# Where the last product of a triple stands in TensorE's order: a gated recurrence followed by a SwiGLU block

## The chip, the cores and the metric

The kernel runs on one core of one Trainium2 chip. The metric is the device time of one execution in microseconds (us); lower is better. TensorE does the matrix products and writes them to PSUM banks, VectorE (DVE in the profile) and ScalarE (ACT) read the banks and do the elementwise work, GpSimd (POOL) and SyncE (SP) mostly issue transfers.

## The reference, cut to what matters

Two layers follow each other. The first is a recurrence over 768 steps for 4 batches of 8 heads, with a state of 48 by 48 per head; the second is a gated feed-forward block over all 3072 tokens.

```python
f = 1 / (1 + exp(-f_logit))                       # (4, 8, 768, 48)
for t in range(768):
    state = f[t, :, None] * state + k[t] v[t]^T
    y[t]  = q[t] @ state
x = y as (3072, 384)
g = x @ w_gate                                    # (384, 1536)
out = (g * sigmoid(g) * (x @ w_val)) @ w_out      # (1536, 384)
```

## The kernel before, in words

The 768 steps are cut into six chunks of 128, so that there are 24 **attention units**, one for each batch and chunk. The feed-forward block takes one chunk of all four batches (512 tokens) at a time. The first chunk goes through plain matrix products; the chunks 1 to 5 go through `mlp_fifteen`, and this is where the change lies. I call the work of `mlp_fifteen(c)` **block c**. In the profile block 1 runs from about 137 to 233 us, block 2 to 327, block 3 to 419, block 4 to 509 and block 5 to the end.

In a block the product with `w_gate` and `w_val` is made by a fast algorithm: both matrices are split in three by three parts, the tokens in three by two, and fifteen products of sums of parts replace eighteen. One **triple** makes those fifteen products for one of four column groups (`NJ` is 4), so a block has four triples, taken in the order 0, 2, 1, 3. Each **product** (`product(r)`, line 1061, r from 0 to 14) is two matrix multiplications of 128x128 by 256 in fp32; a profile shows them as four MATMUL rows and four LDWEIGHTS rows. I write r13 for the product with r = 13, and r0' for the first product of the next triple.

The products go to PSUM tiles by name, as the list `PRODUCTS` says: products 0, 3, 6, 9, 12 and 14 go to one bank "A" and add up there, 1, 4, 7, 10 and 13 to "B", and "o" and "c" take the rest. Between two products that add up in one bank, ScalarE copies the bank out (line 1066: the tiles `c11`, `c22`, `aside` and so on), because each partial sum is needed. VectorE then adds and subtracts these copies (lines 960 and 963). At the end of each of six sums, ScalarE takes the Silu of the gate half (line 1077) and VectorE multiplies it with the value half (line 1013); the products with "A" in the last sum are read from the bank itself. These `finish` steps are put off into the next triple, and those of a block's last triple are made by `finish_late`. Three pools concern us: "A" has two banks, "B" one, and "o" two, which "c" shares; attention units have three banks of their own.

The end of a triple reads

```python
                ("A", "a32", "t11"), ("B", "e1", "t3"), ("A", "a22", "b21")]   # r12, r13, r14
...
                elif r == 12:
                    lag(minus, got[31], got[31], aside("A"))
```

so r14 adds to the bank that r12 wrote, and must come after the copy `aside("A")` of r12. Only r13 lies between.

After the four triples, a block does the product with `w_out` by another fast algorithm of seven products (`down_seven`: `one`, `six`, `two`, `three`, `four`, `five`, `seven`, line 1160, the last at line 1223). Each comes in two halves; a half of `six` is six matrix multiplications of 128x128 by 192, which the profile shows as twelve rows. The first half of `one` or of `six` reads only the hidden tiles of the first two triples.

The order on each engine is written out by hand. `in_turn_of_time` walks over the steps of a block, each with its deemed duration (`PRODUCT` 0.86, half of `DOWN` 1.95), and ahead of a step it puts in every waiting piece whose time has come. `in_order` then fixes this order on each engine. The waiting pieces are those of the attention units of chunk c + 1, with times given by `SCORES`, `CHAINS` and `times`. At a unit's score time these come at once: a Sigmoid of the next unit's gates on ScalarE (line 619), the outputs of the unit before (tiles `y`, lines 745 and 752, and `dS`, line 794), and the scores of the unit itself (tile `sc`, line 701). The scores need two banks, of the pool that `SCORES` names, and VectorE frees them with the causal mask (line 723). Earlier pieces of a unit include the second scan (line 681), the transposition of q (line 685) and the product that gives `qT` (line 593).

A score time `between[n]` falls at the boundary ahead of triple n (counted in order of time), behind r14 of the triple before it.

Of the kernel before, what the change touches and what calls it, by code (L numbers as in the profile page):

```python
# [290 lines left out]
def short_path(ctx, tc, ident, least, judge, q, k, v, f_logit, moe_w_gate, moe_w_val, moe_w_out, out):  # L291
# [12 lines left out]
    NCH = S // C  # L304
# [597 lines left out]
    NJ = NG // 128  # L902

    PRODUCT, DOWN, PLAIN, PLAIN_DOWN = 0.86, 3.9, 2.57, 2.65
# [7 lines left out]
    def chain(k, q, qmul, turn=None, head=None):  # L912
        return (*[k + t for t in STEPS], turn or k + 3.5, head or k + 3.5, q, qmul)

    whole = NJ * TRIPLE + 7 * DOWN
    between = [n * TRIPLE - 0.05 for n in range(NJ)]
    down = [NJ * TRIPLE + n * DOWN / 2 - 0.05 for n in range(14)]
    SCORES = {c: scores for c, scores in zip(range(2, NCH), (
        ((12, "b"), (between[2], "o"), (down[2], "A"), (down[5], "A")),
        ((PRODUCT - 0.05, "b"), (between[1], "o"), (between[3], "o"), (down[3], "A")),  # L920
        *[((down[10] - whole, "A"), (between[1], "o"), (between[3], "o"), (down[3], "A"))] * (NCH - 4)))}
    CHAINS = {c: chains for c, chains in zip(range(2, NCH), (
        (chain(2.6, 4, 8.6), chain(14.5, 20, 23), chain(30, 37, 43.2), chain(57.4, 57.8, 61)),
        (chain(-12, -8.5, -5), chain(3.5, 6, 9), chain(16, 28, 33, 21.5, 23.5), chain(40.1, 53, 55, 44.5, 52)),
        *[(chain(-19.4, -11.2, -9.5), (-7.5, -6.3, 1.3, 2.2, 3.2, 5.5, 8, 10), chain(16, 28, 33, 21.5, 23.5), chain(40.1, 53, 55, 44.5, 52))] * (NCH - 4)))}
    LAST = 72.5

    def times(c):
        at = [t for t, _ in SCORES[c]]
        outputs = [*at[1:], down[10] if c + 1 in SCORES and SCORES[c + 1][0][0] < -1 else LAST]  # L930
        sigmoid = [-14 if c == 3 else SCORES[c - 1][-1][0] - whole - 0.01 if c > 3 else 0, -1.5 if c == 3 else at[0] - 0.01, *[t - 0.01 for t in at[1:]]]
        masks = {"b": 2, "o": 0.9, "A": 1.5}
        return [[f, *steps, s + 0.02, s + masks[kind], s + 2.2, o, o + 0.01, o + 2.1]
                for f, steps, (s, kind), o in zip(sigmoid, CHAINS[c], SCORES[c], outputs)]
# [56 lines left out]
    def down_weight_sums():  # L991
# [4 lines left out]
        for i in (1, 2, 4):  # L996
# [7 lines left out]
    PRODUCTS = [("A", "a11", "t14"), ("B", "a23", "t8"), ("o", "a21", "b22"),  # L1004
                ("A", "a12", "t2"), ("B", "e3", "b32"), ("o", "e0", "t1"),
                ("A", "e5", "t9"), ("B", "e2", "t5"), ("c", "a13", "b11"),
                ("A", "e4", "t4"), ("B", "a33", "t15"), ("c", "a31", "t10"),
                ("A", "a32", "t11"), ("B", "e1", "t3"), ("A", "a22", "b21")]
# [3 lines left out]
    def lag(f, *args):  # L1012
        lagging.append(lambda: f(*args))  # L1013

    def mlp_fifteen(c):
# [113 lines left out]
        hidden_sums, last = down_seven(c, h)  # L1129
        order = list(range(0, NJ, 2)) + list(range(1, NJ, 2))  # L1130
        pieces = [f for j in order for f in triple(j)]
        half = len(PRODUCTS) * (NJ // 2)
        pieces.insert(half + 12, (0, lambda: lag(hidden_sums, 0)))
        pieces += [(0, finish_late), last[0], (0, lambda: lag(hidden_sums, 1))]
        return token_sums, pieces + last[1:]

# [211 lines left out]
    def tokens_of(c):  # L1348
        token_sums, blocks[c] = mlp_fifteen(c)
        token_sums()  # L1350
# [9 lines left out]
def kernel(  # L1360
# [22 lines left out]
    def judge(bank):  # L1383
# [13 lines left out]
        yield  # L1397

    short_path(tc, ident, least, judge, *args)
    with tc.If(redo[0] > 0, label="redo"):  # L1400
        general_path(tc, *args)
# [32 lines left out]
```

## Time and profile before

| quantity | value |
|---|---|
| median of 3 runs | 595.06 us (595.02 to 595.18) |
| the profiled execution's own time | 595.19 us |
| its span in the profile | 593.5 us |
| granted TensorE clock | 0.998 |
| TensorE busy with matmuls, busy with weight loads | 98%, 81% of the span |
| VectorE, ScalarE, GpSimd busy | 80%, 51%, 19% of the span |

A profile row gives an engine, a line of the kernel, an operation, and the tiles out<-in. PE is TensorE's matmul, PEld its weight load, which runs beside the matmul ahead of it. A matmul's start is measured; its end is modelled, so the durations of neighbours overlap. What one product costs is therefore read from the start of one group to the start of the next. "DVE x <- ACT y: 5.0, 19, 0.3" in the list of waits means that DVE stood idle ahead of work on x 19 times, for 5.0 us in all and 0.3 us at most, until ACT had finished y.

### The profile page before, as it was taken

How to read it: one execution, taken by the hardware profiler on the slowest of the kernel's cores; microseconds unless marked ns; L12 is line 12 of the kernel's file. 1: busy time of each engine (PE TensorE's matmuls, PEld its weight loads, DVE VectorE, ACT ScalarE, POOL GpSimd, SP SyncE). 2: the span in 40 equal slices, each digit the busy share in tenths (PEclk: the TensorE clock that was granted, in tenths of full speed). 3: DMA queues.
4: the chain of work that ended last, by engine and by line, in shares of the span. 5: the costliest groups of instructions: out<-in, count | busy, mean ns of one | idle time of the engine just before them, and what ended most of it. 6: DMA issues, size and time to landing. Idle time of an engine off the chain costs nothing.

```text
span 593.5 us, 11514 instructions
## 1 busy us (share of the span) xinstructions
PE 583.6 (98%) x4292; PEld 480.6 (81%) x4292; DVE 477.1 (80%) x826; ACT 303.2 (51%) x567; POOL 112.2 (19%) x240
## 2 busy tenths in 40 slices
PE   8899999999999999999999999999999999999996
PEld 5744445667888999888899888899988899988896
DVE  7978898999989877998986988994978971666631
ACT  3588686024877422676640666631476730355600
POOL 3140345202132240111130030330030330000000
PEclk9999999999999999999999999999999999999999
DMA  9999597333666565552445332544230100100001
GB/s 193 266 309 263 167 229 171 64 99 107 120 120 110 93 149 138 130 109 65 88 117 137 100 81 63 103 109 113 81 92 27 29 11 6 54 1 2 2 0 57
DMA packets 106294, 61.91 MB, mean 104 GB/s; under 512 B 64200, under 2 KB 97032, under 8 KB 106232
## 3 DMA queue, kind: packets, MB, share of 16 engines
q1 hardware_dynamic: 93800, 45.96, 31.8%
q0 software_dynamic: 10992, 13.19, 10.0%
q10 hardware_dynamic: 1440, 1.97, 0.9%
q8 instruction: 35, 0.57, 0.4%
q14 instruction: 27, 0.22, 0.1%
HBM read 47.64 MB, written 8.13 MB: 94 GB/s over the span
## 4 chain that ended last, share of the span: by engine, by line
PE 96%; DVE 2%; ACT 0%; issue 0%; DMA 0%; ACTq 0%; DVEq 0%
PE o L1160 19%; PE A L1061 18%; PE B L1061 15%; PE o L1061 6%; PE c L1061 6%; PE o L868 5%; PE gate L845 5%; PE val L845 5%; PE o L1223 3%; PE sc L701 3%; PE y L745 2%; PE y L774 2%; PE dS L794 2%; PE y L752 1%; PE sc L704 1%; PE kt L708 1%
## 5 line engine op out<-in xcount | busy, mean ns | idle before, releaser
L763 POOL DMA_DIRECT2D xT<-yT x120 | 59.6, 504 | 66.6 <-ACT yT L756 51.4
L1061 PE MATMUL A<-xs,w_both 128*128 128x256 f32 x240 | 62.2, 382 | 0.0
L1160 PE MATMUL o<-w_out,h 128*128 128x192 f32 x360 | 62.0, 327 | 0.0
L1160 PEld LDWEIGHTS o<-w_out,h 128*128 128x128 f32 x360 | 58.7, 190 | 1.2 <-issue 0.7
L1066 ACT COPY aside<-A 128x512 f32<-128x512 f32 x60 | 35.1, 585 | 33.0 <-PE A L1061 32.7
L1066 ACT COPY c<-A 128x512 f32<-128x512 f32 x40 | 23.3, 582 | 55.8 <-PE A L1061 55.8
L960 DVE TENSOR_TENSOR c<-c,aside 128x512 f32<-128x512 f32 x60 | 41.1, 685 | 12.7 <-ACT aside L1066 11.1
L1061 PEld LDWEIGHTS A<-xs,w_both 128*128 128x128 f32 x240 | 44.9, 190 | 6.9 <-issue 1.0
L1013 DVE TENSOR_TENSOR h<-h,c 128x256 f32<-128x256 f32 x100 | 40.5, 413 | 7.6 <-ACT h L1077 7.3
L963 DVE TENSOR_TENSOR c<-c,aside 128x512 f32<-128x512 f32 x60 | 40.9, 682 | 2.8 <-ACT aside L1066 2.8
L1077 ACT ACTIVATE h<-c 128x256 f32<-128x256 f32 x100 | 39.4, 417 | 5.0 <-DVE c L960 3.8
L1160 PE MATMUL o<-ws,h 128*128 128x192 f32 x240 | 41.5, 328 | 0.0
L1061 PE MATMUL B<-xs,w_both 128*128 128x256 f32 x160 | 41.3, 380 | 0.0
L1061 PE MATMUL A<-xs,extra 128*128 128x256 f32 x160 | 41.2, 380 | 0.0
L1061 PE MATMUL B<-xT,extra 128*128 128x256 f32 x160 | 41.1, 379 | 0.0
L1061 PE MATMUL c<-xT,w_both 128*128 128x256 f32 x160 | 41.1, 379 | 0.0
L723 DVE TENSOR_TENSOR A<-sc,causal 128x512 f32<-128x512 f32 x48 | 30.8, 681 | 11.9 <-PE sc L701 11.6
L1066 ACT COPY aside<-B 128x512 f32<-128x512 f32 x60 | 35.1, 585 | 9.0 <-PE B L1061 7.0
L1160 PEld LDWEIGHTS o<-ws,h 128*128 128x128 f32 x240 | 39.1, 190 | 0.7 <-issue 0.7
L963 DVE TENSOR_TENSOR c<-o,c 128x512 f32<-128x512 f32 x40 | 27.3, 684 | 10.9 <-ACT h L1077 6.2
L960 DVE TENSOR_TENSOR c<-c,o 128x384 f32<-128x384 f32 x15 | 8.2, 548 | 34.4 <-PE o L1160 34.4
L1061 PEld LDWEIGHTS B<-xs,w_both 128*128 128x128 f32 x160 | 30.2, 190 | 4.6 <-ACT c L1066 0.4
(165 smaller groups left out, 1211.2 us busy)
## 6 DMA issues: line engine op xcount, KB each, us to landing
fsquares<-in_f_logit_dram SPq DMA_DIRECT2D x64, 96.0 KB, 4.0
qsquares<-in_q_dram SPq DMA_DIRECT2D x64, 96.0 KB, 2.4
ksquares<-in_k_dram SPq DMA_DIRECT2D x64, 96.0 KB, 2.5
w<-in_moe_w_gate_dram SPq DMA_DIRECT2D x6, 768.0 KB
w<-in_moe_w_val_dram SPq DMA_DIRECT2D x6, 768.0 KB, 6.2
w<-in_moe_w_out_dram SPq DMA_DIRECT2D x6, 768.0 KB, 8.4
v<-in_v_dram SPq DMA_DIRECT2D x19, 192.0 KB, 2.9
turn<-ksquares SPq DMA_DIRECT2D x40, 64.0 KB, 2.2
```

The source lines that it names most:

```text
L701: nc.tensor.matmul(sc[par][W * half:W * half + W, a * C:(a + 1) * C], lhsT=kT[r, a, W * half:W * half + W], rhs=qT[r, a, :], start=True, s ...
L723: nc.vector.tensor_tensor(A[:, par], sc[par].rearrange("p (a t) -> p a t", t=C), causal.unsqueeze(1).broadcast_to((128, HP, C)), ALU.mult)
L763: (nc.gpsimd if c >= SQUARES else nc.sync).dma_start(out=xT[c][f % 128:f % 128 + n, f // 128, b * C:(b + 1) * C], in_=yT[r:r + n, par, a / ...
L845: nc.tensor.matmul(p, lhsT=w[:, j, i, :], rhs=xT[c][:, i, :], start=(i == 0), stop=(i == KT - 1))
L868: nc.tensor.matmul(p, lhsT=hidden_tile(h, n // 2)[:, n % 2 * 2 + b // 2, b % 2 * C:(b % 2 + 1) * C], rhs=w_out[:, j, :], start=(n == 0), s ...
L960: nc.vector.tensor_tensor(dst, a, b, ALU.add)
L963: nc.vector.tensor_tensor(dst, a, b, ALU.subtract)
L1013: lagging.append(lambda: f(*args))
L1061: nc.tensor.matmul(p[name][:, n, :], lhsT=weights_of[a][:, n, j, :], rhs=tokens[b], start=fresh and n == 0, stop=True, skip_group_check=True)
L1066: nc.scalar.copy(t, p[name])
L1077: nc.scalar.activation(dst, src[:, 0, :], AF.Silu)
L1160: nc.tensor.matmul(p[:, n, :], lhsT=lhsTs[j][:, n * C:(n + 1) * C], rhs=rhs[:, j, :], start=first and j == order[0] and n == 0, stop=j == ...
```

## The change

It reorders TensorE's work at the ends of triples; no product, copy or transfer is added or removed. At a boundary after n triples that `APART[c]` names, r14 of the old triple and r0' change places. At five boundaries the score time moves from `between[n]` to `inside[n]`, one product earlier, so that the attention unit's matmuls come ahead of r14 and not behind it. At the end of the triples of blocks 2 to 5, the first half of `six` is taken out of the list of the `w_out` halves and put ahead of the last r14.

```diff
     between = [n * TRIPLE - 0.05 for n in range(NJ)]
+    inside = [t - PRODUCT for t in between]
     down = [NJ * TRIPLE + n * DOWN / 2 - 0.05 for n in range(14)]
     SCORES = {c: scores for c, scores in zip(range(2, NCH), (
         ((12, "b"), (between[2], "o"), (down[2], "A"), (down[5], "A")),
-        ((PRODUCT - 0.05, "b"), (between[1], "o"), (between[3], "o"), (down[3], "A")),
-        *[((down[10] - whole, "A"), (between[1], "o"), (between[3], "o"), (down[3], "A"))] * (NCH - 4)))}
+        ((PRODUCT - 0.05, "b"), (between[1], "o"), (inside[3], "o"), (down[3], "A")),
+        *[((down[10] - whole, "A"), (inside[1], "o"), (inside[3], "o"), (down[3], "A"))] * (NCH - 4)))}
...
     LAST = 72.5
+    APART = {1: (1, 3), 2: (1, 2), **{c: (2,) for c in range(3, NCH - 1)}, NCH - 1: range(1, NJ)}
...
         pieces = [f for j in order for f in triple(j)]
-        half = len(PRODUCTS) * (NJ // 2)
-        pieces.insert(half + 12, (0, lambda: lag(hidden_sums, 0)))
+        for n in APART[c]:
+            at = n * len(PRODUCTS)
+            pieces[at - 1], pieces[at] = pieces[at], pieces[at - 1]
+        pieces.insert(len(PRODUCTS) * (NJ // 2) + 12, (0, lambda: lag(hidden_sums, 0)))
+        if c > 1:
+            pieces.insert(-1, last.pop(2))
         pieces += [(0, finish_late), last[0], (0, lambda: lag(hidden_sums, 1))]
         return token_sums, pieces + last[1:]
```

The rows of `SCORES` belong to chunks 2, 3 and then 4 and 5, whose units run in blocks 1, 2, 3 and 4. Block 5 has no attention unit.

## The prediction

> **What bounds the kernel now.** I read the page's busy shares and its chain first.
>
> ```profile
> PE 583.6 (98%) x4292; PEld 480.6 (81%) x4292; DVE 477.1 (80%) x826; ACT 303.2 (51%) x567; POOL 112.2 (19%) x240
> ...
> PE 96%; DVE 2%; ACT 0%; issue 0%; DMA 0%; ACTq 0%; DVEq 0%
> ```
>
> TensorE has nearly all of the chain, so whatever it loses the end loses, and other engines matter only where TensorE waits for them. As matmul ends are modelled, 98% can hide short losses; the weight loads show them. The list of waits, for the weight loads alone, has one line that concerns the products:
>
> ```profile
> PEld A L1061 <- ACT aside L1066: 5.0, 19, 0.3
> ```
>
> The trace has these 19 waits, all ahead of r14: one per triple except the first of block 1. The timeline of one boundary (block 2, third triple next) shows PE, then PEld, then ACT:
>
> ```profile
> 251.02 1.03 PE L1061 MATMUL B<-xs,w_both 128*128 128x256 f32 x4
> ...
> 260.52 1.03 PE L1061 MATMUL A<-xs,w_both 128*128 128x256 f32 x4
> 261.38 1.03 PE L1061 MATMUL B<-xT,extra 128*128 128x256 f32 x4
> 262.28 1.13 PE L1061 MATMUL A<-xT,w_both 128*128 128x256 f32 x4
> 263.25 1.03 PE L1061 MATMUL A<-xs,w_both 128*128 128x256 f32 x4
> ```
> ```profile
> 261.17 0.84 PEld L1061 LDWEIGHTS B<-xT,extra 128*128 128x128 f32 x4
> 262.28 0.73 PEld L1061 LDWEIGHTS A<-xT,w_both 128*128 128x128 f32 x4 [0.27 <-ACT aside L1066]
> ```
> ```profile
> 261.64 0.59 ACT L1066 COPY aside<-A 128x512 f32<-128x512 f32 x1 [0.82 <-PE A L1061]
> ```
>
> Here r12, r13, r14, r0' start at 260.52, 261.38, 262.28, 263.25. ACT was idle, began the copy of r12 as soon as r12 was done, and ended at 262.23; only then did r14's load begin. r13's load had a lead of 0.21 us over its matmul, r14's none.
>
> **The price of one wait.** From 251.02 (r1) to 261.38 (r13) are twelve products: 10.36/12 = 0.863 us each. r13 and r14 together take 263.25 - 261.38 = 1.87. Other boundaries show 1.86 as well (181.24 to 183.10, 546.10 to 547.96), so I take 1.862 - 2 x 0.863 = 0.135 us: about 0.03 is r14's late start, and 0.105 is its slow first step. This, not the 0.27 us of the load's idle time, is what TensorE loses, since a load normally runs 0.21 us ahead.
>
> **What the Trainium skill says.** "TensorE: Matmul & The Clock Gate", section "Step-by-step: what each phase is for": TensorE pulls a weight load ahead of matmuls in flight, while matmuls stay in order. The trace agrees: 0.21 us of lead, lost when the load waits. "PSUM — Partial Sum Buffer", section "Terms": two engines may not be on the same bank and quadrant at once. That is why r14 must wait for a reader of bank A though it adds to it; the trace shows the wait. "ScalarE: Activation LUTs", section "What ACT_TABLE_LOAD costs", gives about 1.283 us for a table load; the table loads for Silu have exactly 1283 ns here.
>
> **The change, part by part.** Of the 19 waits I go through those that it touches.
>
> Plain swaps: block 1 before its fourth triple; block 2 before its second and third; blocks 3 and 4 before the third; block 5 before the third and fourth. That is 1 + 2 + 2 + 2 = 7 waits. With r0' between, r14 comes 1.73 us after r12's end, and the copy needs about 0.85 (261.38 to 262.23). r0' needs the other bank A, last read by DVE's multiplication (line 1013): of the first triple in block 2 that ends at 260.22, and r0' is wanted at 262.25, so 2.0 us are left (2.5 in block 1, where it ends at 179.58). r0' brings ScalarE one more copy (c11, 0.58 us) ahead of r14, and r14 has none, so r1' finds bank B two products after r13, as before. I cost the swap at nothing on this cover; if it failed, the cost would be up to the 0.135 gained. At block 2's second triple the unit stays between r0' and r14.
>
> Unit ahead of r14: one boundary in block 2, two each in blocks 3 and 4: 5 waits. TensorE's changes of shape stay the same in number. The first product after scores is dear anyway, because its load has no lead:
>
> ```profile
> 249.07 1.05 PE L701 MATMUL sc<-qT,kT 48*64 48x128 f32 x32
> 250.06 1.13 PE L1061 MATMUL A<-xs,w_both 128*128 128x256 f32 x4
> 251.02 1.03 PE L1061 MATMUL B<-xs,w_both 128*128 128x256 f32 x4
> ```
>
> that is 0.96 for r0'. Now r14 pays this 0.10 and r0' doesn't, and r14's own 0.135 goes. The unit issues all its work 1.0 us earlier: y, dS and scores on PE, the Sigmoid and two yT copies on ACT, six xT transfers on POOL, and the v load and mostly one kt transfer on SP. r14 has no such work, so it is moved past nothing on ACT, POOL and SP. Two things could be late. The scores need bank "o", freed by DVE's subtraction from c, which ends at 338.86 and 431.44 ahead of the second triple of blocks 3 and 4, while scores would start about 340.6 and 432.7; the least slack is 1.2 us. qT is ready even earlier. And yT may wait for the Sigmoid behind a table load (1.28 + 0.63 us), about 0.5 us; nothing on PE waits for it soon.
>
> Half of `six` ahead of r14: blocks 2 to 5, 4 waits. PE has the same rows; a product beside w_out rows costs no more than usual (block 4 enters its first product at 419.11 after 24 rows from 415.21, 3.90 us as elsewhere). The half issues nothing to other engines. What moves with it is DVE's order in blocks 2 to 4: the second scan and the transposition of q, due at 52 and 53, now come ahead of the last triple's multiplications. At the end of block 2 DVE does now:
>
> ```profile
> 292.38 0.69 DVE L960 TENSOR_TENSOR c<-c,aside 128x512 f32<-128x512 f32 x1
> 293.56 1.09 DVE L1013 TENSOR_TENSOR h<-h,c 128x256 f32<-128x256 f32 x3 [0.48 <-ACT h L1077]
> 294.57 0.41 DVE L1013 TENSOR_TENSOR h<-h,A 128x256 f32<-128x256 f32 x1
> 294.90 1.23 DVE L681 TENSOR_TENSOR_SCAN gates<-gates,start 128x516 f32<-128x516 f32 x1
> 296.04 0.68 DVE L685 STREAM_TRANSPOSE tails<-qsquares 128x512 f32<-128x512 f32 x1
> ```
>
> After the change: sum to 293.07, scan and transposition (1.23 + 0.68) to about 294.9, first multiplication to 295.3. Its tile is wanted by the second half of `one`, in its second third. That half starts at 291.57 + 1.95 + 0.86 + 1.95 = 296.3, the third at 297.0, its load at 296.8: 1.5 us of slack. Bank A of r14 is read later, but its next user, the scores before the second half of `six`, comes 3.9 us after r14. The transposition's q load is issued with the transfers of a unit earlier, some 20 us ahead by the schedule, so SP is no cover that could go.
>
> The first swap in block 1 gains nothing: scores and the kt transposition already lie ahead of r14 there, and r14 takes one usual step:
>
> ```profile
> 152.12 1.03 PE L1061 MATMUL A<-xT,w_both 128*128 128x256 f32 x4
> 152.99 1.03 PE L1061 MATMUL A<-xs,w_both 128*128 128x256 f32 x4
> ```
>
> Block 5's first swap meets the small `row` transposition ahead of r14: it sits inside the wait today, and must be paid by itself then (0.11 us by its start-to-start), so I count 0, with 0.13 as the upper end. Two waits in block 1 (third triple, end) stay.
>
> **Sum.** (7 + 5 + 4) x 0.135 = 2.16 us. The profiled execution took 595.19 (span 593.5 and 1.7 around it) and would take 593.0; it stood 0.13 above the median of 595.06, so for a median I say 595.06 - 2.16 = **592.9 us**.
>
> **The rivals.** First, the new places take waits of their own in the nine boundaries with an attention unit or w_out: then only the swaps pay, 7 x 0.135 = 0.95, time 594.1. For it speaks that DVE is busy 82.0 of 93 us in block 1 and 81.5 of 94 in block 2; against it the slacks of 1.2 us and more. Second, the change doesn't do what it says: the slow first step belongs to r14 itself, and only the late start of 0.03 goes: 16 x 0.03 = 0.5, time 594.6. The 0.87 us of r14 at 152.12 speaks against it. Third, on the other side: DVE becomes the bound at the ends of blocks 2 to 4. The scan and transposition stand ahead of the multiplications, and if DVE reaches them late, `one` stops for its hidden tile. It starts to cost once DVE is 1.5 us later than worked out and ends slower than before by 0.2% once that is 2.6 us, (2.16 + 1.19)/3 beyond the slack. If the slack is gone altogether, three blocks pay 1.91 us each: 592.9 + 5.7 = 598.6. For it speaks the strict order in DVE's queue; against it that the same pieces run now without a wait before them.
>
> **How the numbers follow.** A measurement of this kernel can tell about 0.2%, 1.19 us, from no change. All sixteen waits go: 0.86, with 592.3 to 593.5 as its own range (the two ends are `row` and some 0.4 us of three other products that wait for a ScalarE copy in block 1's second triple, and a quarter of the gain lost). Only the swaps pay: 0.05. Only late starts go: 0.03. DVE at the block ends: 0.06. The first is faster by over 0.2%, the next two within it, the last slower: 0.86, 0.08, 0.06. The range reaches from 592.3 to the swaps' case, 594.2.
>
> **What would show it.** In the profile after, the line of waits for `aside` should fall from 19 to two of 0.27 us and perhaps one short one; r14 behind r0' should take 0.863 and behind scores 0.97; PE should show the same rows. A new PEld wait of r0' on a multiplication, of `sc` on a subtraction or of `o` on `h` would show the rivals, and a span that shrinks by less than 1.2 us would make the forecast wrong.

## The result, and the profile after

The changed kernel takes 592.87 us (median of 6 runs, 592.80 to 593.02), the kernel before, run again beside it, 595.08 (594.97 to 595.26). The ratio is 0.9963, with a 95% interval of 0.9950 to 0.9976. The profiled execution took 593.02, with a span of 591.3 at a granted clock of 0.999.

The page's busy shares and chain look as before:

```profile
PE 580.7 (98%) x4292; PEld 481.9 (81%) x4292; DVE 477.4 (81%) x826; ACT 302.8 (51%) x567; POOL 112.3 (19%) x240
...
PE 96%; DVE 2%; DMA 1%; ACT 0%; issue 0%; SPq 0%; ACTq 0%; DVEq 0%
```

TensorE has the same 4292 rows and the same share of a shorter span. The shares can't tell where the time went. The list of waits of the weight loads can (us in all, times, longest):

```profile
PEld A L1063 <- ACT yT L756: 0.7, 4, 0.2
...
PEld A L1063 <- ACT aside L1068: 0.5, 2, 0.3
```

The 19 waits for `aside` have become two, both in block 1. The four for `yT` are r14 behind the scores of a unit, 0.17 us each (at two more such places the 0.17 is put down to issue); r0' showed the same 0.17 at these six places before, all put down to issue. The load of whatever follows scores has no lead. The timeline of the boundary that the prediction showed (block 2, third triple next), PE, then PEld, then ACT:

```profile
260.27 1.03 PE L1063 MATMUL A<-xs,w_both 128*128 128x256 f32 x4
261.13 1.03 PE L1063 MATMUL B<-xT,extra 128*128 128x256 f32 x4
261.99 1.03 PE L1063 MATMUL A<-xs,w_both 128*128 128x256 f32 x4
262.86 0.81 PE L1063 MATMUL A<-xT,w_both 128*128 128x256 f32 x3
```
```profile
262.64 0.84 PEld L1063 LDWEIGHTS A<-xT,w_both 128*128 128x128 f32 x4
```
```profile
261.38 0.59 ACT L1068 COPY aside<-A 128x512 f32<-128x512 f32 x1 [0.82 <-PE A L1063]
```

r12, r13, r0', r14 now start 0.86 to 0.87 apart. The copy of r12 ends at 261.97, and r14's load begins at 262.64, 0.22 ahead of its matmul: a lead like any other's. Where a unit comes first, r14 pays the slow first step that r0' paid before:

```profile
248.82 1.05 PE L701 MATMUL sc<-qT,kT 48*64 48x128 f32 x32
249.80 1.13 PE L1063 MATMUL A<-xT,w_both 128*128 128x256 f32 x4
250.77 1.03 PE L1063 MATMUL B<-xs,w_both 128*128 128x256 f32 x4
```

And at the end of block 2, with the half of `six` between:

```profile
290.17 1.03 PE L1063 MATMUL B<-xT,extra 128*128 128x256 f32 x4
291.04 2.11 PE L1166 MATMUL o<-ws,h 128*128 128x192 f32 x12
292.99 1.03 PE L1063 MATMUL A<-xT,w_both 128*128 128x256 f32 x4
293.85 4.06 PE L1166 MATMUL o<-w_out,h 128*128 128x192 f32 x24
```

that is 0.87 + 1.95 + 0.86 from r13 to `one`, with nothing lost.

Since TensorE hardly ever idles, the time by blocks shows the gain place by place. I read a block from the start of its first product to the start of the next block's first product in the timeline; for block 5 the end is the start of its last group (line 1223 before, 1229 after), because the last stores behind that point take 8.8 to 9.0 us in one execution or another.

| block | before | after | gain | waits taken away x 0.135 |
|---|---|---|---|---|
| 1 | 94.63 | 94.51 | 0.12 | 1: 0.135 |
| 2 | 93.82 | 93.28 | 0.54 | 4: 0.54 |
| 3 | 92.59 | 92.05 | 0.54 | 4: 0.54 |
| 4 | 89.60 | 89.06 | 0.54 | 4: 0.54 |
| 5 | 75.74 | 75.31 | 0.42 | 3: 0.405 |

The sum is 2.16 to 2.17.

### The profile page after: what moved, and what is told of

It is laid out like the page before. It is cut to its first block, busy times and chain, and to the rows that moved or that the text cites. A ratio compares the mean times of both kernels' runs of the same rounds, so it can differ in the third digit from the quotient of the medians.

```text
span 591.3 us, 11514 instructions
## 1 busy us (share of the span) xinstructions
PE 580.7 (98%) x4292; PEld 481.9 (81%) x4292; DVE 477.4 (81%) x826; ACT 302.8 (51%) x567; POOL 112.3 (19%) x240
## 4 chain that ended last, share of the span: by engine, by line
PE 96%; DVE 2%; DMA 1%; ACT 0%; issue 0%; SPq 0%; ACTq 0%; DVEq 0%
PE o L1166 19%; PE A L1063 18%; PE B L1063 15%; PE o L1063 6%; PE c L1063 6%; PE o L868 5%; PE gate L845 5%; PE val L845 5%; PE o L1229 3%; PE sc L701 3%; PE y L745 2%; PE y L774 2%; PE dS L794 2%; PE y L752 1%; PE sc L704 1%; PE kt L708 1%
```

## The experiments

The theory: each of sixteen waits for the copy of r12 is worth 0.135 us, wherever it lies, and the new places have slack enough. The rivals: the new places take waits of their own, only the late start goes, or VectorE becomes the bound at the block ends.

### One kind of move at a time

Four kernels take one part each of the change. The first has the swaps that end a wait and nothing else:

```diff
-    APART = {1: (1, 3), 2: (1, 2), **{c: (2,) for c in range(3, NCH - 1)}, NCH - 1: range(1, NJ)}
+    APART = {1: (3,), 2: (1, 2), **{c: (2,) for c in range(3, NCH - 1)}, NCH - 1: (2, 3)}
...
-        ((PRODUCT - 0.05, "b"), (between[1], "o"), (inside[3], "o"), (down[3], "A")),
+        ((PRODUCT - 0.05, "b"), (between[1], "o"), (between[3], "o"), (down[3], "A")),
...
-        if c > 1:
-            pieces.insert(-1, last.pop(2))
```

> Only the seven swaps of r14 and r0' that take away a wait; no unit and no half of six moved. Theory (each wait gone is worth 0.135 us, wherever it is): 7 x 0.135 = 0.95 us less than before, span near 592.5, 12 waits for aside left. Rival (only the late start of 0.03 goes, the slow first step belongs to r14): 0.2 us less.

The second keeps the moved units, with an empty `APART` and no half of `six`:

> Only the five attention units moved ahead of r14, no swap, no half of six. Theory: 5 x 0.135 = 0.68 us less than before, span near 592.8, 14 waits for aside left; r14 behind the scores takes 0.97 and r0' 0.863. Rival (the unit takes a wait of its own for bank o, qT or kt): no gain, new waits of sc or y in the list.

The third keeps the half of `six` alone:

> Only the first half of six moved ahead of the last r14 in blocks 2 to 5. Theory: 4 x 0.135 = 0.54 us less than before, span near 592.9, 15 waits for aside left. Rival (VectorE reaches the last multiplications late, now behind the scan and the transposition): blocks 2 to 4 gain nothing or lose, with a wait of the second half of one on h.

The fourth has `APART = {1: (1,), 5: (1,)}` and nothing else:

> Only the two swaps to which the forecast gave nothing: the first of block 1 and the first of block 5. Theory: 0 to 0.13 us less than before, with block 1 unchanged. Rival (the first swap of block 1 relieves ScalarE, and the three products that wait for a copy in its second triple wait less): up to 0.4 us less, all of it in block 1.

Measured, as gains in us by block, read in the same way (a block that a kernel leaves alone repeats within 0.02):

| kernel | block 1 | 2 | 3 | 4 | 5 | sum | waits for `aside` left | median, ratio to before |
|---|---|---|---|---|---|---|---|---|
| swaps | 0.13 | 0.27 | 0.14 | 0.14 | 0.27 | 0.95 | 12 | 594.17, 0.9986 (0.9979 to 0.9992) |
| units | -0.01 | 0.14 | 0.28 | 0.27 | 0.00 | 0.68 | 14 | 594.31, 0.9988 (0.9981 to 0.9994) |
| half of `six` | 0.01 | 0.14 | 0.14 | 0.14 | 0.13 | 0.56 | 15 | 594.68, 0.9993 (0.9985 to 1.0001) |
| two idle swaps | 0.00 | 0.00 | 0.00 | 0.00 | 0.02 | 0.02 | 18 | 594.99, 1.0000 (0.9991 to 1.0008) |

Every block gains a multiple of 0.135 us, by the number of waits taken away in it, and the parts add up to the whole (2.2 us). No place is worth less than another, so the first rival falls, and with 0.135 and not 0.03 for each so does the second. For the half of `six` and for the idle swaps, the runs' intervals alone can't tell a gain from none; the blocks in the traces can, as they repeat so closely. The first swap of block 1 gives nothing, and ScalarE's waits in that block's second triple stay. That of block 5 gives 0.02, since the `row` transposition, inside the wait before, is now paid by itself.

### The copy of r12 made twice

ScalarE copies r12 into the same tile a second time, in the kernel before and in the changed one:

```diff
-                    lag(minus, got[31], got[31], aside("A"))
+                    t = aside("A")
+                    nc.scalar.copy(t, p["A"])
+                    lag(minus, got[31], got[31], t)
```

> The kernel before, with ScalarE's copy of r12 made twice into the same tile: it ends some 0.5 us later (the pitch of such copies in a row). Theory (r14 waits for this copy in 19 triples, with nothing to cover it): 19 x 0.48 = 9 us more, about 604, and waits of 0.75 us each. Rival (r14's loss is its own and the copy only ends at the same time): no change.

> The changed kernel, with the copy of r12 made twice. Theory (one product between gives the load 0.67 us more than the copy needs, the unit and the half of six give more): only the two waits left in block 1 grow, 2 x 0.48 = 1 us more than the changed kernel, about 593.9. Rival (the cover is thinner than worked out, or the delay goes on to bank B, whose copy comes next): the swaps wait again, up to 9 us more.

The kernel before with it takes 606.9 us, ratio 1.020 (1.017 to 1.023); its timeline (ACT, then PE) has

```profile
264.15 0.59 ACT L1066 COPY aside<-A 128x512 f32<-128x512 f32 x1 [0.82 <-PE A L1061]
264.77 0.59 ACT L1114 COPY aside<-A 128x512 f32<-128x512 f32 x1
```
```profile
265.41 1.13 PE L1061 MATMUL A<-xT,w_both 128*128 128x256 f32 x4 [0.48 <-ACT aside L1114]
```

The second copy starts 0.62 us after the first and not 0.48. It writes the same tile and reads the same bank as the first; which of the two makes it later was not tried. So the span grows by 11.5 us (593.5 to 605.0), which over 19 waits is 0.61 each, and not by 9. The sign and the mechanism are as expected: r14 follows the end of that copy one to one.

The changed kernel with it takes 594.07, ratio to the kernel before 0.9982 (0.9975 to 0.9990), and within the five blocks this is the one wait for which the list shows more time:

```profile
PEld A L1063 <- ACT aside L1116: 1.8, 2, 0.9
```

Blocks 2, 3 and 4 take 93.28, 92.05 and 89.06 us, the changed kernel's times to the last digit, and block 1 takes 1.23 us more, twice 0.615. One product of cover thus holds at least 0.62 us, of the 0.67 that the prediction's times leave.

### VectorE made late at the block ends

Operations on a constant tile, which keep its values, are put ahead of the last triple's multiplications in blocks 2 to 4:

```diff
+        if 1 < c < NCH - 1:
+            pieces.append((0, lambda: [nc.vector.tensor_tensor(floor, floor, floor, ALU.max) for _ in range(2)]))
         pieces += [(0, finish_late), last[0], (0, lambda: lag(hidden_sums, 1))]
```

> The changed kernel, with two more VectorE operations on 128x516 (some 0.6 us each) ahead of the last triple's multiplications in blocks 2 to 4. Theory (1.5 us of slack at this place): no change, 592.9. Rival (VectorE is nearly the bound there): 0.3 to 1.2 us more per block, 594 to 596.5.

> The same with five such operations, some 3.05 us. Theory (slack 1.5): the second half of one waits 1.55 us plus 0.1 for the lost lead in three blocks, 4.8 us more than the changed kernel, about 597.7. Rival (no slack): 9.2 us more. Rival (the tile is wanted later than worked out): no change.

With two, the time is 593.03 (ratio to the kernel before 0.9966, 0.9952 to 0.9979) and blocks 2 to 4 are unchanged. With five it is 598.16, slower than the kernel before (1.0052, 1.0029 to 1.0075). The list of waits and the timeline of block 2 of that kernel:

```profile
PEld o L1168 <- DVE h L1015: 5.6, 3, 1.9
```
```profile
298.18 1.08 PE L1168 MATMUL o<-w_out,h 128*128 128x192 f32 x5 [1.57 <-DVE h L1015]
```

The five operations take 3.5 us, not 3.05 (each starts 0.70 after the last, on its result). The matmul is due at 293.85 + 1.95 + 0.65 = 296.45 and comes at 298.18, 1.73 late; each of the three blocks is 1.83 us longer, 1.73 plus 0.10 for the lost lead. So 3.48 - 1.73 = 1.75 us of VectorE's delay were covered at the matmul, or 1.54 at its load: the 1.5 of the prediction. The third rival is a real mechanism, and the changed kernel stands 1.5 us away from it.

### The two waits left in block 1

The half of `six` is left out in block 1. The next kernel drops the condition:

```diff
-        if c > 1:
-            pieces.insert(-1, last.pop(2))
+        pieces.insert(-1, last.pop(2))
```

> The changed kernel, with the half of six ahead of the last r14 in block 1 too. Its weight sum ws comes by a transfer that is issued at 189.8 and lands some 6.9 us later, at about 196.7, while the half would start at 194.2. Theory: TensorE waits there for the transfer, 2.5 us more in block 1 less the 0.135 gained, about 595.2. Rival (the weights are there in time): 0.135 less, 592.7.

It is slower than the kernel before: 597.01, ratio 1.0039 (1.0025 to 1.0054); its four runs lie near 596.0 and near 598.1, two each, of which more below. The profile of one near 596.0 shows

```profile
196.92 2.19 PE L1165 MATMUL o<-ws,h 128*128 128x192 f32 x12 [1.71 <-DMA ws<-w_out]
```

The half would start at 195.04 (I had taken r13's start), so the wait is 1.9 us and not 2.5. A second loss of 1.2 us comes later: the last unit's scores wait longer for `qT`. Block 1 takes 97.55 us, 3.04 more.

The next kernel takes the first half of `five`, whose weights are there, and swaps r14 and r0' ahead of block 1's third triple as well (`five` then keeps its bank under a name of its own):

```diff
-    APART = {1: (1, 3), ...
+    APART = {1: (1, 2, 3), ...
...
-        if c > 1:
-            pieces.insert(-1, last.pop(2))
+        pieces.insert(-1, last.pop(2 if c > 1 else 10))
```

> The changed kernel, with the two waits left in block 1 taken away as well: r14 and r0' change places ahead of the third triple, and the first half of five (whose weights landed at about 189) comes ahead of the last r14. Theory: no wait for aside left, 2 x 0.135 = 0.27 us less in block 1, about 592.6. Rival (five so early holds a bank o that another product wants, or its hidden sums are late): block 1 no shorter, with a new wait of o.

No wait for `aside` is left, yet the median is 594.02 (0.9988 of before, 0.9980 to 0.9995), over a microsecond above the changed kernel's. It missed what I expected, and the new wait of "o" that my rival had is not there either. The timeline of PE and the busy time of one stretch (TensorE's granted clock is the value after POOL's) say why:

```profile
212.34 1.10 PE L701 MATMUL sc<-qT,kT 48*64 48x128 f32 x32 [1.46 <-DVE qT L593]
213.38 5.85 PE L1165 MATMUL o<-w_out,h 128*128 128x192 f32 x24
```
```profile
213.00:219.00 6.00, 6.00 (x42) 5.83 (x33) 2.87 (x5) 0.30 (x2) 4.94 (x10) 0.72 0.69 180
```

The scores start 2.12 us after the step before them (210.22), which takes 0.49 where nothing waits: 1.63 us are lost, most of it idle. Soon after it the granted clock was 0.72 over 6 us; cut into slices of 1 us, the same view has 0.50 in each from 214 to 217, and 1.00 from 213 to 213.5 and from 218 on. In this stretch `two` took 5.68 us (213.38 to 219.06), where a later kernel takes 4.00. Five of the 15 runs have a mean clock of 0.996 and 595.4 to 595.6 us, as the profiled one; the others have 0.998 or more and 593.8 to 594.3. The two runs near 598.1 of the kernel with the half of `six` in block 1 have 0.996 too. So the late scores cost 1.23 us more than in the changed kernel (which loses 0.40 there), and the cut clock 1.7 us in one run of three, going by the mean clocks of the runs that have no trace.

I then formed another theory: the idle time has its cause in VectorE's order. `one`'s second half now comes behind a unit, and the two subtractions that follow it (1.8 us, wanted by no product before `three`) fell into the stretch where VectorE makes the last unit's `qT`. The last kernel but one keeps both moves and puts the subtractions behind the first half of `two` in block 1; the last takes the third swap alone, added to the changed kernel:

```diff
             if part:
                 nc.scalar.copy(kept["u"], kept["p"])
-                for odd in range(2):
-                    lag(minus, h[odd][:, :, 0, :], s1[odd], h[odd][:, :, 0, :])
+                if c > 1:
+                    first_differences()
...
         def two(part):
+            if part == 0 and c == 1:
+                first_differences()
```

> As with the half of five ahead of the last r14 in block 1 and the third swap, but the two subtractions of 128x768 that follow the second half of one (1.8 us on VectorE, wanted by three alone) come behind the first half of two in block 1. Theory (it was these two, moved in front of the last unit's scan and products by the new order, that made its qT late and TensorE idle for 1.6 us): qT is ready at about 210.4, the idle time goes, TensorE's clock is not cut, and block 1 takes 94.24 or up to 0.4 less; 592.2 to 592.6. Rival (qT was late for another reason): block 1 stays over 95.5, about 594.

> The changed kernel, with r14 and r0' changing places ahead of block 1's third triple too; the end of block 1 stays. Theory: one wait for aside left, 0.135 us less in block 1 (94.37 for 94.51), about 592.7. Rival (the moved r14 disturbs ScalarE's or VectorE's order in block 1 as the half of five did): block 1 no shorter.

The first of them takes **592.03 us**, ratio 0.9948 (0.9935 to 0.9962), a little under the 592.2 to 592.6 that I expected. On VectorE, then on PE, its timeline has

```profile
209.79 0.69 DVE L593 TENSOR_TENSOR qT<-tails,gates 128x512 f32<-128x512 f32 x1
211.81 1.29 DVE L723 TENSOR_TENSOR A<-sc,causal 128x512 f32<-128x512 f32 x2 [1.33 <-PE sc L701]
```
```profile
210.73 1.05 PE L701 MATMUL sc<-qT,kT 48*64 48x128 f32 x32
```

`qT` ends at 210.48, before the scores want it, and all five runs have a mean clock of 0.998 or more. Block 1 takes 93.78, 0.73 less than in the changed kernel: 0.27 for the two waits, 0.40 for a wait of these scores that the changed kernel has too (its scores come 0.89 after the step before), and the rest, 0.06, for the scores' slow first step behind that. The third swap alone gives 592.75 (0.9962, 0.9948 to 0.9975) and 94.36 in block 1, 0.15 less. So the kernel with all the moves and the later subtractions is 0.8 us faster than the changed kernel; for the third swap alone only the trace shows a gain, as its runs (592.67 to 593.19) overlap those of the changed kernel.

## Why the prediction was right, point by point

**The bound and the price.** TensorE's order was what mattered, and 0.135 us for each wait, read from start to start, is what the blocks gave: 0.54 in each of three blocks with four waits. The idle time in the list (0.27 each, 5.0 in all) would have promised twice that.

**The count.** 7 + 5 + 4 waits, each kind run by itself, gave 0.95, 0.68 and 0.56, where the sum had 0.95, 0.68 and 0.54. The first swap of block 1 was put at nothing and gave nothing. `row` in block 5, left at 0 with 0.13 as the upper end, gave 0.02.

**What was costed at nothing.** The cover of a swap, 0.67 us by the prediction's times, held a copy 0.62 us later. The slack on VectorE at the block ends, 1.5 us by the prediction, is 1.54 at the load. That the order there changes as worked out is seen in VectorE's timeline of the changed kernel at the end of block 2:

```profile
291.86 0.69 DVE L962 TENSOR_TENSOR c<-c,aside 128x512 f32<-128x512 f32 x1
292.47 1.23 DVE L681 TENSOR_TENSOR_SCAN gates<-gates,start 128x516 f32<-128x516 f32 x1
293.61 0.69 DVE L685 STREAM_TRANSPOSE tails<-qsquares 128x512 f32<-128x512 f32 x1
294.22 1.05 DVE L1015 TENSOR_TENSOR h<-h,c 128x256 f32<-128x256 f32 x3
```

The scan and the transposition stand ahead of the multiplications, as the prediction had it. The slack for bank "o" and for the Sigmoid ahead of `yT` was not tried by delaying them; no wait of scores on a subtraction appears in the list, and the units gave their full gain.

**The sum.** 592.9 was forecast and 592.87 measured, inside the likeliest case's own range of 592.3 to 593.5. The line of waits fell from 19 to two, without the one more that was allowed for. What the Trainium skill says in "TensorE: Matmul & The Clock Gate", section "Step-by-step: what each phase is for", on loads pulled ahead of matmuls fits the price: of the 0.135 us, the trace puts 0.105 on the slow first step of a product whose load had no lead. The rule on PSUM banks that the prediction gives as the reason for the wait was not needed for it: the copy must hold the sum without r14, so r14 has to come behind it in any case, and no run tells the two reasons apart.

## What to carry to other kernels

Where one engine is busy from end to end, price a wait by the distance of the starts around it against the undisturbed distance, not by the idle time of a load that normally runs ahead; then count the places, and check for each move how much slack the new neighbours have. A reordering of the bound engine also reorders the queues of the others, as pieces are emitted with its steps: what is not wanted soon must not slip in front of what is. A move that is right by itself can lose more there than it gains, as the half of `five` did until two subtractions were moved out of its way.

## What the runs showed that I had not expected

An idle time of about 1.5 us on TensorE was followed, in one run of three, by a clock at half for some 3.4 us (0.50 from 214 to 217 us in the trace), which cost 1.7 us: more than the idle time itself. The Trainium skill, "TensorE: Matmul & The Clock Gate", section "Why this matters for your kernels", warns of gaps over some 3 us; here the cut came at times behind a gap of half that. That the gap brings the cut is inferred from the two standing together, and from the clock staying whole in the five runs of the kernel without the gap. The length of the gap alone seems not to decide it: ten of those 15 runs kept a mean clock of 0.998 or more, and the kernel with five late VectorE operations has three gaps of 1.57 us in its trace, while its three runs have mean clocks of 0.999 and 1.000. There the gaps lie between matmuls of `one`, while the gap ahead of the cut lies within an attention unit, among its smaller matmuls; whether that makes the difference was not tried.

In two places, operations in a row that touch the tile that the last one wrote came dearer: 0.62 us from start to start for the doubled copy on ScalarE, where other work follows such a copy after 0.49 (261.38 to 261.87 in the changed kernel), and 0.70 for VectorE on 128x516, where 0.61 separates the sum and the scan in the changed kernel (291.86 to 292.47). That the shared tile is the cause is not shown, as the operations compared differ in other ways too.
